# Token rows of a top-2 expert layer: scaled and turned in one fp32 product, with a new order of expert 0's preparation

## The chip, the cores and the metric

One core of a Trainium2 chip runs the kernel in one launch. The metric is the device time of one execution in microseconds (us), as the median of several.

## What is computed

Attention of 4 batches, 8 heads, 768 positions and head size 64, over 96 local and 8 global keys, gives `x` of 3072 tokens by 512. A gate then picks two of eight experts for each token, and each expert is a two-layer network:

```python
noisy_logits = x @ w_gate + np.log1p(np.exp(x @ w_noise)) * noise
...
for e in range(E):                       # 8 experts
    for k in range(2):
        mask = top2[:, k] == e
        h = np.maximum(x[mask] @ w1[e], 0.0)                     # 512 -> 1024
        out[mask] += top2_w[mask, k, None] * (h @ w2[e])         # 1024 -> 512
```

## The kernel before

**Attention** goes over 96 pairs of heads (24 blocks of 128 tokens, four pairs each) in one unrolled loop, `n` (lines 746 to 767). The order of all work is written by hand: an engine takes its instructions in the order in which the program emits them. The table `at(step, function, ...)` hangs other work on the end of a step: loads of weights (`load_w`), the weight scales of expert 0 (`scales(0)`, steps 36 to 70), its first weight matrix (`split(0, 1, j)`, steps 74 to 88) and the first tiles of tokens (`ready(0, t)`, from step 92).

**Routing** (`route`, line 289) goes over five segments of the 24 blocks, woven into the loop. Each ends in scatters that write (token, weight) entries into one list per expert in DRAM, by POOL, two for each block (line 382). After the third segment POOL loads expert 0's list (line 391, tile `tb0`) and gathers its first four tiles of 128 rows (line 219).

**Experts.** Each takes 812 rows: four tiles of 128 (part 0 of `xh`, `xl`) and three of 100 (part 1). Every operand is held as two fp16 parts, a high one and the rest, and a product is three fp16 products. `up(e, c, f)` is one of eight 128-wide slices of the hidden layer for part c (12 matmuls), `down(e, t)` a tile of 128 rows (24 matmuls of 512 columns), `down_t(e, d)` a quarter of the features for all 300 other rows (24 matmuls of 300 columns), and `back` turns the latter to rows again. `put` writes rows out by a POOL scatter (line 807). A generator per expert, `prep(e)`, yields after each step of weight preparation: in `scales` eight maxima on DVE (line 147), a product that turns them (line 151) and one that spreads them (line 159), then 16 `split`s, each an ACT and a DVE step (lines 199, 204). `step(e, n)` advances it, between the products of the expert before.

**Tokens.** `gather` brings a tile of rows (`xg`, five buffers). `ready` (line 230) reduces each row to its sum of magnitudes, makes a power of two from it in four small DVE steps, and writes the scaled row as two fp16 parts, by ACT (line 240) and DVE (line 241), into `xp`. `turn` (line 243) turns these with eight fp16 transposes of 128 (or 100) columns into one PSUM bank; ACT copies the high half to `xh`, DVE the low half to `xl`. `ready` of a tile stands two blocks ahead of its `turn` in experts 1 to 6 (lines 924 to 933), and one ahead in the stretch of `down_t(0, j)` (lines 892 to 899).

Of the kernel before, what the change touches and what calls it, by code (L numbers as in the profile page):

```python
# [20 lines left out]
P = 128  # L21
NP = 96
TA = 4
# [11 lines left out]
def tile_local_global_attention_then_moe(  # L35
# [46 lines left out]
    def bank16(tag, bufs):  # L82
        return psum.tile([P, 1024], F16, name=tag, tag=tag, bufs=bufs)

# [6 lines left out]
    ident16 = consts.tile([P, P], F16, name="ident16")  # L91
    exa = consts.tile([P, E, TA], F32, name="exa")
    exb = consts.tile([MB, E, TB], F32, name="exb")
# [46 lines left out]
    def scales(e):  # L140
# [14 lines left out]
        dg = small.tile([8, 8], F32, name="dg")  # L155
        nc.vector.tensor_scalar(dg, ident[:8, :8], mc, TINY, op0=OP.mult, op1=OP.max)
# [24 lines left out]

    def weigh_a(e):
        nc.vector.scalar_tensor_tensor(yra[:, e], (tba[:, e] if e else tb0)[:, :, 1].bitcast(F32), fac[:, e:e + 1],
                                       exa[:, e], op0=OP.mult, op1=OP.mult)

    def weigh_b(e):
        nc.vector.scalar_tensor_tensor(yrb[:, e], tbb[:, e, :, 1].bitcast(F32), fac[:MB, e:e + 1], exb[:, e],
                                       op0=OP.mult, op1=OP.mult)
# [19 lines left out]
    xg, xp = {}, {}  # L208
# [17 lines left out]
    def spare_bank(make=bank):  # L226
        spare[0] += 1
        return make("m" if spare[0] % 2 else "lg", 1)

    def ready(e, t):  # L230
        x = xg.pop((e, t))
        m = x.shape[0]
        c, s, u = (gp.tile([m, 1], F32, name=f"{n}{m}", bufs=2) for n in ("l1", "pw", "up"))
        ex = exa[:, e, t:t + 1] if t < TA else exb[:, e, t - TA:t - TA + 1]
        nc.vector.tensor_reduce(c, x, op=OP.add, axis=AX.X, apply_absolute_value=True)
        nc.vector.tensor_scalar(c, c, TINY, None, op0=OP.max)
        power(ex, c, s)
        nc.vector.tensor_scalar(u, s, 2.0 ** (X_UP - 1), None, op0=OP.mult)  # L238
        xp[e, t] = gp.tile([m, 2 * Dm], F16, name="xp", bufs=3)
        nc.scalar.activation(xp[e, t][:, :Dm], x, AF.Copy, scale=u)  # L240
        nc.vector.scalar_tensor_tensor(xp[e, t][:, Dm:], x, u, xp[e, t][:, :Dm], op0=OP.mult, op1=OP.subtract)

    def turn(e, t, ps=None):
        x = xp.pop((e, t))
        m = x.shape[0]
        c, c0 = (0, t * P) if t < TA else (1, (t - TA) * MB)
        ps = (spare_bank(bank16) if ps is None else ps)[:, :2 * KC * m].rearrange("p (k t) -> p k t", k=2 * KC)
# [153 lines left out]
    with ExitStack() as actx:  # L401
# [108 lines left out]
        def gate_consts():  # L510
            nc.vector.tensor_copy(ident16, ident)
# [196 lines left out]
        else:  # L708
# [37 lines left out]
            for n in range(NPAIR + LAG):  # L746
# [9 lines left out]
                if n >= NPAIR - 1:  # L756
                    t = n - NPAIR + 1
                    turn(0, t, bank16("sc", 2))
                    if t == 2:
                        turn(0, 3, bank16("sc", 2))  # L760
# [11 lines left out]
    with ExitStack() as mctx:  # L772
# [43 lines left out]
        def down(e, t):  # L816
# [32 lines left out]
        for f in range(FC):  # L849
# [6 lines left out]
            if f == 0:  # L856
                load_w()
# [5 lines left out]
        for t in range(TB):  # L863
            gather(0, TA + t)
        ahead = {e: prep(e) for e in range(1, E)}

        def step(e, n):
# [5 lines left out]
        for t in range(TA - 1):  # L873
            down(0, t)
            step(1, [3, 3, 2][t])
            ready(0, TA + t)
        for t in range(TB):
            turn(0, TA + t, bank16("sc", 2) if t == TB - 1 else None)
        for t in range(3):
            gather(1, t)  # L880
        down(0, TA - 1)
        step(1, 1)
        for f in range(FC):
            up(0, 1, f)
            step(1, 1)
            if f % 2 and f < 6:
                ready(1, f // 2)
                gather(1, 3 + f // 2)
            if f % 2 == 0 and f:
                turn(1, f // 2 - 1)  # L890
        ready(1, 3)
        for j in range(KC):
            down_t(0, j)
            if j == 0:
                gather(1, 6)
            if j < 3:
                ready(1, 4 + j)
            turn(1, 3 + j)
            step(1, 2)
        weigh_b(0)  # L900
        for e in range(1, E):
            last = e + 1 == E
            for f in range(FC):
# [3 lines left out]
                step(e, 4)  # L907
                step(e + 1, 1)
# [15 lines left out]
            for j, (f, t) in enumerate(steps_t + steps if last else steps + steps_t):  # L924
                f(e, t)
                if not last:
                    step(e + 1, [2, 2, 2, 3, 1, 1, 1, 1][j])
                    if j < TA + TB - 2:
                        ready(e + 1, j + 2)
                    if j < TA + TB:  # L930
                        turn(e + 1, j)
                        if j < 2:
                            gather(e + 1, 5 + j)
                elif j in (KC, KC + 1, KC + 2):
# [85 lines left out]
```

## Time and profile before

| | us |
|---|---|
| median of three executions (850.0 to 852.4) | 851.05 |
| the profiled execution | 852.33 |
| its span, first to last instruction | 850.2 |
| TensorE (PE) busy | 782.8 |
| VectorE (DVE) busy | 502.5 |
| ScalarE (ACT) busy | 391.5 |
| GpSimd (POOL) busy | 236.6 |

Busy time of PE contains the latency of each instruction, so what a group costs PE is the time from its start to the start of the next. The clock column of a stretch is the mean granted TensorE clock as a share of 2.4 GHz, and 0.50 is 1.2 GHz. In a timeline the bracket gives the idle time of the engine before the row and what ended it.

### The profile page before, as it was taken

Reading aid. Unit: us, or ns where it says so; the run is one execution under the profiler, and the core shown is the slowest. Engines: PE = TensorE matmul, PEld = TensorE weight load, DVE = VectorE, ACT = ScalarE, POOL = GpSimd, SP = SyncE. Lnnn points to the kernel's source line nnn. Section 1 sums busy time; section 2 is a strip of 40 time slices with the busy share of each in tenths; the row PEclk is TensorE's granted clock in tenths of the full one; section 3 lists DMA queues with packets and bytes.
Section 4 is the critical chain, followed back from the end, with each engine's and each line's share of the span. In section 5 each row is a group of like instructions: output and inputs, shape, how many; then the busy total and the mean of one; then the engine's idle time right before and its main releaser. Section 6 shows DMA issues by size and latency. Waiting matters only on the chain. (4 is left out here: it accounts for less than half of the span.)

```text
span 850.2 us, 14911 instructions
## 1 busy us (share of the span) xinstructions
PE 782.8 (92%) x5513; PEld 535.7 (63%) x5513; DVE 502.5 (59%) x1594; ACT 391.5 (46%) x792; POOL 236.6 (28%) x225
## 2 busy tenths in 40 slices
PE   7999999995598467999999999999999999999994
PEld 6999998995543245465564655656565565665662
DVE  6456766752664557867667666756766766663200
ACT  5777676783341234435424524533542543353211
POOL 4000050586264320404223141240413214122013
PEclk9999999998599599999999999999999999999997
DMA  9899698672436422707423541750643344032014
GB/s 215 230 265 284 180 191 227 166 175 65 134 113 147 83 54 79 201 8 173 114 69 95 162 99 34 185 119 20 160 122 75 94 125 89 7 64 30 1 22 61
DMA packets 86667, 100.77 MB, mean 119 GB/s; under 512 B 35626, under 2 KB 48170, under 8 KB 86586
## 3 DMA queue, kind: packets, MB, share of 16 engines
q1 hardware_dynamic: 71322, 73.05, 31.2%
q0 software_dynamic: 15264, 26.69, 16.8%
q8 instruction: 45, 0.74, 0.4%
q14 instruction: 36, 0.29, 0.1%
HBM read 71.46 MB, written 28.24 MB: 117 GB/s over the span
## 5 line engine op out<-in xcount | busy, mean ns | idle before, releaser
L788 PEld LDWEIGHTS <-w1h 128*128 128x128 f16 x1024 | 100.0, 99 | 70.8 <-issue 0.8
L240 ACT ACTIVATE xp<-xg,up 128x512 f16<-128x512 f32 (+1 forms) x56 | 40.4, 722 | 152.3 <-DVE up L238 109.7
L807 POOL DMA_INDIRECT out_dram<-y,tba x28 | 44.6, 1593 | 234.7 <-ACT y L806 234.7
L822 PE MATMUL av<-w2h,hh 128*128 128x512 f16 x256 | 98.1, 383 | 0.0
L822 PE MATMUL av<-w2l,hh 128*128 128x512 f16 x256 | 98.0, 383 | 0.0
L822 PE MATMUL av<-w2h,hl 128*128 128x512 f16 x256 | 98.0, 383 | 0.0
L572 DVE CUSTOM_DVE_ANT_0 ns<-sc,bias 128x168 f32<-128x168 f32 (+1 forms) x192 | 55.6, 321 | 62.1 <-PE sc L569 31.9
L576 ACT ACTIVATE a<-ns,mx 128x168 f32<-128x168 f32 (+1 forms) x192 | 72.7, 423 | 42.1 <-DVE mx L572 41.4
L382 POOL DMA_INDIRECT tbl<-ent,sli x48 | 48.4, 1008 | 142.0 <-DVE sli L377 129.3
L788 PE MATMUL at<-xh,w1h 128*128 128x512 f16 (+1 forms) x256 | 86.7, 338 | 0.0
L788 PE MATMUL sc<-xh,w1h 128*128 128x512 f16 (+1 forms) x256 | 86.5, 338 | 0.0
L788 PE MATMUL at<-xl,w1h 128*128 128x512 f16 (+1 forms) x256 | 86.3, 337 | 0.0
L788 PE MATMUL sc<-xl,w1h 128*128 128x512 f16 (+1 forms) x256 | 86.2, 337 | 0.0
L788 PE MATMUL at<-xh,w1l 128*128 128x512 f16 (+1 forms) x256 | 86.1, 337 | 0.0
L788 PE MATMUL sc<-xh,w1l 128*128 128x512 f16 (+1 forms) x256 | 86.1, 336 | 0.0
L822 PEld LDWEIGHTS <-hh 128*128 128x128 f16 x512 | 49.8, 99 | 55.3 <-issue 2.2
L807 POOL DMA_INDIRECT out_dram<-y,tbb x24 | 38.1, 1588 | 151.8 <-ACT y L806 151.4
L147 DVE TENSOR_REDUCE wmx<-raw 128x1 f32<-128x1024 f32 x64 | 76.9, 1208 | 0.0
L569 PE MATMUL sc<-ks,qbuf 128*128 128x168 f32 (+1 forms) x384 | 71.0, 310 | 5.6 <-DMA qbuf<-in_q 5.6
L798 ACT ACTIVATE hh<-at 128x300 f16<-128x300 f32 (+1 forms) x62 | 31.3, 505 | 96.5 <-PE at L788 96.5
L832 PE MATMUL av<-hh,w2h 128*128 128x300 f16 x256 | 74.6, 292 | 0.0
L788 PEld LDWEIGHTS <-w1l 128*128 128x128 f16 x512 | 50.2, 98 | 38.5 <-issue 0.5
(163 smaller groups left out, 1623.5 us busy)
## 6 DMA issues: line engine op xcount, KB each, us to landing
raw<-in_w SPq DMA_DIRECT2D x32, 1024.0 KB
out_dram<-zero SPq DMA_DIRECT2D x14, 512.0 KB
vs<-in_v SPq DMA_DIRECT2D x24, 260.0 KB
qbuf<-in_q SPq DMA_DIRECT2D x48, 128.0 KB
xd<-xr SPq DMA_DIRECT2D x24, 256.0 KB
ks<-in_k SPq DMA_DIRECT2D x20, 272.0 KB
vp<-in_v SPq DMA_DIRECT2D x20, 195.0 KB
ks<-in_k SPq DMA_DIRECT2D x4, 464.0 KB
```

The source lines that it names most:

```text
L147: nc.vector.tensor_reduce(m[:, i:i + 1], t[:, i % 2 * n:(i % 2 + 1) * n], op=OP.max, axis=AX.X, apply_absolute_value=True)
L240: nc.scalar.activation(xp[e, t][:, :Dm], x, AF.Copy, scale=u)
L382: ins = nc.gpsimd.indirect_dma_start(out=tbl, out_offset=bass.IndirectOffsetOnAxis(ap=sli[:, i, j:j + 1], axis=0), in_=ent[:, i, j], in_of ...
L569: nc.tensor.matmul(ps[:, s], qs[b, j][:, 2 * i0 + s, hp], ks[b, j][:, hp, k0:k0 + w], start=True, stop=True)
L572: nc.vector.tensor_tensor_reduce(out=ns[:, s, :w], in0=ps[:, s], in1=bias[:, hp, s] if i else bias0[:, hp, s], scale=-scale, scalar=3e38, ...
L576: nc.scalar.activation(A[n][:, s, c:c + w], ns[:, s, :w], AF.Exp, bias=mx[:, s:s + 1], scale=-1.0)
L788: nc.tensor.matmul(ps, w[e % 2][:, k, fs], x[c][:, k], start=n == 0, stop=n == 3 * KC - 1)
L798: nc.scalar.activation(hh[c][:, f], ps, AF.Relu)
L807: ins = nc.gpsimd.indirect_dma_start(out=out, out_offset=bass.IndirectOffsetOnAxis(ap=r[:, 0:1], axis=0), in_=y, in_offset=None, bounds_ch ...
L822: nc.tensor.matmul(ps, x[0][:, f, cols], w[e % 2][:, f], start=n == 0, stop=n == 3 * FC - 1)
L832: nc.tensor.matmul(ps, w[e % 2][:, f, cols], x[1][:, f], start=n == 0, stop=n == 3 * FC - 1)
```

## The change

`ready` no longer makes fp16 parts. After the reduction and two small DVE steps, POOL writes a diagonal matrix `dg`, the identity scaled by the rows' powers of two. `turn` multiplies the gathered fp32 rows with it: four fp32 matmuls, whose result is turned and scaled. ACT takes the high part from PSUM, DVE the rest (PSUM less high part). `xg` is held until `turn`. `scales` loses two of its yields, and so has ten. Expert 0's loads, scales and first weight matrix stand earlier among the attention steps, and the steps around expert 0 and between the experts are in another order.

```diff
@@ scales
         nc.tensor.transpose(ps[:8, :P], m, ident)
-        yield
         mc = small.tile([8, 1], F32, name="mc")
...
-        nc.tensor.matmul(ps[:, :8], one8, dg, start=True, stop=True)
-        yield
+        nc.tensor.matmul(ps[:, :8], one8, d8, start=True, stop=True)
@@ weigh_a and weigh_b
+    def weigh(e, y, c, w):
+        nc.vector.tensor_scalar(c[:, e].bitcast(I32), c[:, e].bitcast(I32), EXP, None, op0=OP.bitwise_and)
+        nc.vector.scalar_tensor_tensor(y[:, e], w.bitcast(F32), fac[:w.shape[0], e:e + 1], c[:, e],
+                                       op0=OP.mult, op1=OP.mult)
@@ ready
-        x = xg.pop((e, t))
+        x = xg[e, t]
...
         nc.vector.tensor_reduce(c, x, op=OP.add, axis=AX.X, apply_absolute_value=True)
         nc.vector.tensor_scalar(c, c, TINY, None, op0=OP.max)
-        power(ex, c, s)
-        nc.vector.tensor_scalar(u, s, 2.0 ** (X_UP - 1), None, op0=OP.mult)
-        xp[e, t] = gp.tile([m, 2 * Dm], F16, name="xp", bufs=3)
-        nc.scalar.activation(xp[e, t][:, :Dm], x, AF.Copy, scale=u)
-        nc.vector.scalar_tensor_tensor(xp[e, t][:, Dm:], x, u, xp[e, t][:, :Dm], op0=OP.mult, op1=OP.subtract)
+        nc.vector.tensor_scalar(s.bitcast(I32), c.bitcast(I32), EXP, EXP, op0=OP.bitwise_and, op1=OP.bitwise_xor)
+        dg[e, t] = gp.tile([m, m], F32, name="dg", bufs=3)
+        nc.gpsimd.tensor_scalar(dg[e, t], ident[:m, :m], s, 2.0 ** (X_UP - 1), op0=OP.mult, op1=OP.mult)
@@ turn
-        for k in range(2 * KC):
-            nc.tensor.transpose(ps[:, k], x[:, k * P:(k + 1) * P], ident16[:m, :m])
+        for k in range(KC):
+            nc.tensor.matmul(ps[:, k], x[:, k * P:(k + 1) * P], d, start=True, stop=True)
         cols = slice(c0, c0 + m)
-        nc.scalar.activation(xh[c][:, :, cols], ps[:, :KC], AF.Copy)
-        nc.vector.tensor_copy(xl[c][:, :, cols], ps[:, KC:])
+        nc.scalar.activation(xh[c][:, :, cols], ps, AF.Copy)
+        nc.vector.tensor_sub(xl[c][:, :, cols], ps, xh[c][:, :, cols])
@@ attention
-            for j in 20, 26, 32, 56, 84, 90:
+            for j in 20, 26, 32, 38, 76, 84, 90:
                 at(j, load_w)
             first = scales(0)
-            for j in 36, 39, 42, 45, 48, 51, 62, 64, 66, 67, 68, 69, 70:
+            for j in 28, 30, 35, 37, 44, 46, 50, 52, 54, 55:
                 at(j, lambda: next(first, 0))
             for j in range(FC):
-                at(74 + 2 * j, split, 0, 1, j, nc.gpsimd)
+                at(56 + 2 * j, split, 0, 1, j, nc.gpsimd)
             for t in range(TA):
-                at(NPAIR - 4 + t, ready, 0, t)
+                at(NPAIR - 3 + min(t, 2), ready, 0, t)
@@ down, and expert 0's up
-        def down(e, t):
+        def down(e, t, between={}):
...
+                    if n in between:
+                        turn(e, between[n], bank("sc", 2) if n > 20 else None)
...
-            if f == 0:
-                load_w()
@@ around expert 0
-        for t in range(TA - 1):
-            down(0, t)
-            step(1, [3, 3, 2][t])
-            ready(0, TA + t)
-        for t in range(TB):
-            turn(0, TA + t, bank16("sc", 2) if t == TB - 1 else None)
-        for t in range(3):
-            gather(1, t)
-        down(0, TA - 1)
-        step(1, 1)
+        for t in range(TA):
+            down(0, t, {13: TA, 18: TA + 1, 22: TA + 2} if t == TA - 1 else {})
+            step(1, 2)
+            if t == TA - 2:
+                for j in range(TB):
+                    ready(0, TA + j)
+        step(1)
+        for t in range(2):
+            ready(1, t)
+        for t in range(2, 5):
+            gather(1, t)
         for f in range(FC):
             up(0, 1, f)
-            step(1, 1)
-            if f % 2 and f < 6:
-                ready(1, f // 2)
-                gather(1, 3 + f // 2)
-            if f % 2 == 0 and f:
-                turn(1, f // 2 - 1)
-        ready(1, 3)
+            if f in (0, 1, 3, 5, 7):
+                step(1)
+            if f in (2, 4):
+                ready(1, 2 + f // 4)
+            if f > 3:
+                turn(1, f - 4)
+                if f < 6:
+                    gather(1, f + 1)
         for j in range(KC):
             down_t(0, j)
-            if j == 0:
-                gather(1, 6)
-            if j < 3:
-                ready(1, 4 + j)
-            turn(1, 3 + j)
-            step(1, 2)
+            step(1)
+            if j < TB:
+                ready(1, TA + j)
+                turn(1, TA + j)
@@ experts 1 to 7, second half of up
             for f in range(FC):
                 up(e, 1, f)
-                step(e + 1, f > 0)
-                if not last and f > 5:
-                    ready(e + 1, f - 6)
+                if f < 2:
+                    step(e + 1)
+                if not last and f in (4, 6):
+                    ready(e + 1, f // 2 - 2)
```

Three places where the instructions move follow. Line numbers of the change are those of its own file, and a number behind a name tells buffers of one name apart.

POOL's queue at the third segment's scatters (`sli_2783` before, `sli_2798` now), expert 0's list (`tb`) and its first gathers. Before:

```order
L382 DMA tbl<-ent_2783,sli_2898 25600x2 x2
L201 TENSOR_SCALAR raw<-raw,wsc 128x4x128
L202 TENSOR_TENSOR w1l_103<-raw,w1h_101 128x4x128
L382 DMA tbl<-ent_2783,sli_2898 25600x2 x8
L391 DMA tb_97<-tbl 128x8
L201 TENSOR_SCALAR raw<-raw,wsc 128x4x128
L202 TENSOR_TENSOR w1l_103<-raw,w1h_101 128x4x128
L201 TENSOR_SCALAR raw<-raw,wsc 128x4x128
L202 TENSOR_TENSOR w1l_103<-raw,w1h_101 128x4x128
L219 DMA xg<-xd,tb_97 128x512 x4
```

Now:

```order
L198 TENSOR_SCALAR raw<-raw,wsc 128x4x128
L199 TENSOR_TENSOR w1l_102<-raw,w1h_100 128x4x128
L377 DMA tbl<-ent_2306,sli_2506 25600x2 x12
L377 DMA tbl<-ent_2798,sli_2910 25600x2 x10
L386 DMA tb_96<-tbl 128x8
L216 DMA xg<-xd,tb_96 128x512 x4
L236 TENSOR_SCALAR dg<-ident,pw_3312 128x128
```

The eight pairs of the weight step (`raw`, `w1l`) that stood among the scatters and behind the list's load now stand ahead of the second and third segments' scatters, and the list's load and the gathers follow the last scatter directly.

DVE's queue at `down_t(0, 0)` to `down_t(0, 1)`: `yt` is the copy of a transposed down product, `w1l` the DVE step of `split`, `xl` the low part of a turn, the reduction of `xg` the first step of `ready`. Before:

```order
L252 COPY xl_106<-lg 128x4x128
L204 SCALAR_TENSOR_TENSOR w1l_104<-raw,wsc,w1h_102 128x4x128 x2
L835 COPY yt<-av 128x300
L235 TENSOR_REDUCE l_4332<-xg 100x1
L236 TENSOR_SCALAR l_4332<-l_4332 100x1
L179 TENSOR_SCALAR exb<-l_4332 100x1
L180 TENSOR_SCALAR pw_4333<-exb 100x1
L238 TENSOR_SCALAR up_4334<-pw_4333 100x1
L241 SCALAR_TENSOR_TENSOR xp<-xg,up_4334,xp 100x512
L252 COPY xl_3496<-m 128x4x100
L204 SCALAR_TENSOR_TENSOR w1l_104<-raw,wsc,w1h_102 128x4x128
```

Now:

```order
L201 SCALAR_TENSOR_TENSOR w1l_103<-raw,wsc,w1h_101 128x4x128
L232 TENSOR_REDUCE l1b<-xg 100x1
L233 TENSOR_SCALAR l1b<-l1b 100x1
L234 TENSOR_SCALAR pw_4191<-l1b 100x1
L247 TENSOR_TENSOR xl_3460<-m,xh_3459 128x4x100
L831 COPY yt<-av 128x300
L201 SCALAR_TENSOR_TENSOR w1l_103<-raw,wsc,w1h_101 128x4x128
L232 TENSOR_REDUCE l1b<-xg 100x1
L233 TENSOR_SCALAR l1b<-l1b 100x1
L234 TENSOR_SCALAR pw_4232<-l1b 100x1
L247 TENSOR_TENSOR xl_3460<-lg,xh_3459 128x4x100
```

Before, `ready` of a tile stands ahead of the `xl` of the tile before it, so that it runs one turn ahead; now each tile's `ready` stands behind the weight step and directly ahead of its own turn.

PE's queue in the second up half of expert 1: `wmx` are the eight maxima of expert 2's weights, `at` and `sc` the banks of slices f = 0 and f = 1. Before:

```order
L788 LDWEIGHTS w1l_104
L788 MATMUL sc<-xh_3495,w1l_104 128x300
L151 MATMUL m<-ident,wmx 8x128
L788 LDWEIGHTS w1h_102
L788 MATMUL at<-xh_3495,w1h_102 128x300
```

Now:

```order
L782 LDWEIGHTS w1l_103
L782 MATMUL at<-xh_3459,w1l_103 128x300
L147 MATMUL m<-ident,wmx 8x128
L782 LDWEIGHTS w1h_101
L782 MATMUL sc<-xh_3459,w1h_101 128x300
```

The product that turns the maxima stood behind slice f = 1 and now stands behind slice f = 0. On DVE the last maximum is still emitted with slice f = 7 of the first half.

## Rows read from the trace of the kernel before

**Rows 1.** The page's part 1: busy us (share of the span) and instructions of each engine, whole span.

```profile
PE 782.8 (92%) x5513; PEld 535.7 (63%) x5513; DVE 502.5 (59%) x1594; ACT 391.5 (46%) x792; POOL 236.6 (28%) x225
```

**Rows 2.** Busy time of each engine in eight stretches: from:to, length, then busy us (instructions) of PE, PEld, DVE, ACT and POOL, the granted TensorE clock as a share of full speed, DMA share, GB/s. The stretches are the last attention steps (200 to 219), the turns of expert 0's first tiles (219 to 233), the first half of expert 0's up projection (233 to 258.4), three of its four down products (258.4 to 274), the turns of its last three tiles and the fourth down product (274 to 298), the second half of its up projection (298 to 322.8), its transposed down products (322.8 to 340.6), and the 500 us of experts 1 to 7 that follow.

```profile
200.00:219.00 19.00, 3.25 (x30) 3.01 (x27) 4.12 (x26) 2.09 (x5) 12.91 (x11) 0.68 0.26 76
219.00:233.00 14.00, 11.47 (x87) 10.74 (x88) 9.16 (x37) 5.93 (x12) 0.00 (x0) 0.50 0.40 132
233.00:258.40 25.40, 24.29 (x121) 11.09 (x121) 17.09 (x64) 11.82 (x22) 16.89 (x16) 0.91 0.36 98
258.40:274.00 15.60, 15.60 (x73) 6.93 (x71) 4.88 (x6) 1.89 (x3) 4.51 (x5) 1.00 0.69 171
274.00:298.00 24.00, 10.72 (x50) 4.83 (x50) 12.52 (x26) 4.60 (x8) 9.41 (x8) 0.64 0.45 89
298.00:322.80 24.80, 16.57 (x125) 11.68 (x124) 14.04 (x39) 9.69 (x18) 5.91 (x5) 0.93 0.21 47
322.80:340.60 17.80, 14.83 (x131) 10.65 (x129) 13.10 (x35) 8.88 (x17) 0.00 (x0) 1.00 0.30 106
340.60:840.60 500.00, 493.90 (x3142) 292.12 (x3139) 301.03 (x635) 204.62 (x365) 125.81 (x94) 1.00 0.38 89
```

**Rows 3.** The timeline of POOL's queue, start us, duration us, engine, line, operation [idle before <-releaser]: the first scatter of the second routing segment, the last scatter of the third, the load of expert 0's list, and the first gather of its rows.

```profile
156.96 0.98 POOL L382 DMA_INDIRECT tbl<-ent,sli  x1 [35.56 <-DVE sli L377]
...
197.79 0.97 POOL L382 DMA_INDIRECT tbl<-ent,sli  x1 [0.30 <-issue]
...
204.07 0.60 POOL L391 DMA_DIRECT2D tb<-tbl  x1 [5.32 <-DMA tbl<-ent,sli]
...
210.47 1.12 POOL L219 DMA_INDIRECT xg<-xd,tb  x1 [0.16 <-issue]
```

**Rows 4.** The timeline of DVE and PE, same columns: the slots of the third segment are ready; the first row of `ready`; PE's first product after its wait; expert 0's first up product.

```profile
177.67 0.17 DVE L377 CAST sli<-sl 128x10 int32<-128x10 f32 x1
...
214.00 0.69 DVE L235 TENSOR_REDUCE l<-xg 128x1 f32<-128x512 f32 x1 [13.88 <-DMA xg<-xd,tb]
...
219.12 0.69 PE L270 MATMUL m<-ident,xr 128*128 128x128 f32 x2 [15.87 <-DVE xr L617]
...
232.98 0.63 PE L788 MATMUL at<-xh,w1h 128*128 128x512 f16 x1
```

**Rows 5.** Groups of instructions of one line and one shape: line, engine, operation, out<-in, shapes, count | busy us, mean ns of one | idle time of the engine before them. Lines 235 and 238 are in `ready`, 147 in `scales`, 199 and 204 the two steps of `split`, 201 its first step on POOL, 799 a read from PSUM less an fp16 part, 837 the copy of a transposed down product.

```profile
L235 DVE TENSOR_REDUCE l<-xg 100x1 f32<-100x512 f32 x24 | 16.3, 678 | 11.2 <-DMA xg<-xd,tbb 11.2
...
L238 DVE TENSOR_SCALAR up<-pw 100x1 f32<-100x1 f32 x24 | 3.7, 153 | 0.8
...
L147 DVE TENSOR_REDUCE wmx<-raw 128x1 f32<-128x1024 f32 x64 | 76.9, 1208 | 0.0
...
L199 ACT ACTIVATE w1h<-raw,wsc 128x512 f16<-128x512 f32 x64 | 44.2, 712 | 0.0
...
L204 DVE SCALAR_TENSOR_TENSOR w1l<-raw,wsc,w1h 128x512 f16<-128x512 f32 x56 | 40.8, 748 | 11.7 <-ACT w1h L199 9.6
...
L201 POOL TENSOR_SCALAR raw<-raw,wsc 128x512 f32<-128x512 f32 x8 | 12.7, 1586 | 0.2
...
L799 DVE SCALAR_TENSOR_TENSOR hl<-sc,hh 128x512 f16<-128x512 f32 x30 | 20.7, 691 | 31.8 <-ACT hh L798 31.8
...
L837 ACT ACTIVATE yt<-av 128x300 f32<-128x300 f32 x16 | 6.6, 414 | 8.4 <-PE av L832 8.4
```

**Rows 6.** The timeline of PE, same columns, in pairs of a group and its successor: an fp16 turn of 128 rows and the next product; one of 100 rows and the next; an fp32 product of 128 columns (two instructions, four records) and the next; an fp32 product of 65 columns with 128x128 weights (one instruction, two records) and the next.

```profile
452.14 0.61 PE L249 MATMUL m<-ident,xp 128*128 128x128 f16 x8
...
452.59 0.38 PE L822 MATMUL av<-w2h,hh 128*128 128x512 f16 x1
...
472.54 0.52 PE L249 MATMUL m<-ident,xp 100*128 100x100 f16 x8
...
472.90 0.29 PE L832 MATMUL av<-hh,w2h 128*128 128x300 f16 x1
...
52.19 0.61 PE L569 MATMUL sc<-ks,qbuf 128*128 128x128 f32 x4
...
52.64 0.33 PE L608 MATMUL av<-vp,at 104*128 104x65 f32 x2
...
194.19 0.39 PE L608 MATMUL av<-vs,at 128*128 128x65 f32 x2
...
194.41 0.39 PE L608 MATMUL av<-vp,at 104*128 104x65 f32 x2
```

**Rows 7.** Waits of PE's weight loads from 360 us to the end: line <- what it waited for: us in total, times, longest.

```profile
PEld L249 <- issue: 5.3, 6, 0.9
...
PEld m L159 <- DVE dg L156: 1.5, 6, 0.2
```

**Rows 8.** The timeline of PE and DVE, same columns, in expert 1: the first product of its second up half, the last of the next expert's eight weight maxima, and the product that turns those maxima.

```profile
434.17 0.29 PE L788 MATMUL at<-xh,w1h 128*128 128x300 f16 x1
...
435.61 1.21 DVE L147 TENSOR_REDUCE wmx<-raw 128x1 f32<-128x1024 f32 x1
...
437.24 0.27 PE L151 MATMUL m<-ident,wmx 128*8 128x128 f32 x1
```

**Rows 9.** The timeline of POOL and PE, same columns: the first gather of expert 0's last three tiles, and the first turn of one of them.

```profile
271.59 1.11 POOL L219 DMA_INDIRECT xg<-xd,tbb  x1 [10.17 <-DMA tbb<-tbl]
...
277.58 0.35 PE L249 MATMUL m<-ident,xp 100*128 100x100 f16 x4 [3.50 <-ACT xp L240]
```

More of the change, by code (lines that the diff above doesn't have):

```diff
@@ L90, in tile_local_global_attention_then_moe @@
     ident = consts.tile([P, P], F32, name="ident")
-    ident16 = consts.tile([P, P], F16, name="ident16")
-    exa = consts.tile([P, E, TA], F32, name="exa")
-    exb = consts.tile([MB, E, TB], F32, name="exb")
+    l1a = consts.tile([P, E, TA], F32, name="l1a")
+    l1b = consts.tile([MB, E, TB], F32, name="l1b")
     wmx = consts.tile([P, 2, 8], F32, name="wmx")
@@ L151, in scales @@
         nc.tensor.transpose(ps[:8, :P], m, ident)
-        yield
         mc = small.tile([8, 1], F32, name="mc")
         nc.vector.tensor_reduce(mc, ps[:8, :P], op=OP.max, axis=AX.X)
-        dg = small.tile([8, 8], F32, name="dg")
-        nc.vector.tensor_scalar(dg, ident[:8, :8], mc, TINY, op0=OP.mult, op1=OP.max)
+        d8 = small.tile([8, 8], F32, name="d8")
+        nc.vector.tensor_scalar(d8, ident[:8, :8], mc, TINY, op0=OP.mult, op1=OP.max)
         yield
         ps = bank("m", 1)
-        nc.tensor.matmul(ps[:, :8], one8, dg, start=True, stop=True)
-        yield
+        nc.tensor.matmul(ps[:, :8], one8, d8, start=True, stop=True)
         m2 = small.tile([P, 2], F32, name="m2")
@@ L206, in split @@
             load_w()
-    xg, xp = {}, {}
+    xg, dg = {}, {}
     def rows(e, t):
@@ L510, in gate_consts @@
         def gate_consts():
-            nc.vector.tensor_copy(ident16, ident)
             nc.vector.memset(one8, 1.0)
@@ L757, in tile_local_global_attention_then_moe @@
                     t = n - NPAIR + 1
-                    turn(0, t, bank16("sc", 2))
+                    turn(0, t, bank("sc", 2))
                     if t == 2:
-                        turn(0, 3, bank16("sc", 2))
+                        turn(0, 3, bank("sc", 2))
                 if LAG <= n:
@@ L864, in tile_local_global_attention_then_moe, with step @@
             gather(0, TA + t)
+        for t in range(2):
+            gather(1, t)
         ahead = {e: prep(e) for e in range(1, E)}
-        def step(e, n):
+        def step(e, n=1):
             for _ in range(n):
@@ L872, in tile_local_global_attention_then_moe @@
         weigh_a(0)
[L873 to L879 removed]
+        for t in range(TA):
[5 more added lines that the diff above has]
+        step(1)
+        for t in range(2):
+            ready(1, t)
+        for t in range(2, 5):
             gather(1, t)
[L881 to L882 removed]
         for f in range(FC):
             up(0, 1, f)
[L885 to L891 removed]
+            if f in (0, 1, 3, 5, 7):
[6 more added lines that the diff above has]
+                    gather(1, f + 1)
         for j in range(KC):
             down_t(0, j)
[L894 to L899 removed]
+            step(1)
+            if j < TB:
+                ready(1, TA + j)
+                turn(1, TA + j)
         weigh_b(0)
@@ L906, in tile_local_global_attention_then_moe @@
                     back(e - 1, f)
-                step(e, 4)
-                step(e + 1, 1)
+                if f < 4:
+                    step(e, 2 if e == 1 else 1)
+                step(e + 1)
             if not last:
@@ L915, in tile_local_global_attention_then_moe @@
                 up(e, 1, f)
-                step(e + 1, f > 0)
-                if not last and f > 5:
-                    ready(e + 1, f - 6)
+                if f < 2:
+                    step(e + 1)
+                if not last and f in (4, 6):
+                    ready(e + 1, f // 2 - 2)
             if not last:
@@ L926, in tile_local_global_attention_then_moe @@
                 if not last:
-                    step(e + 1, [2, 2, 2, 3, 1, 1, 1, 1][j])
                     if j < TA + TB - 2:
@@ L933, in tile_local_global_attention_then_moe @@
                             gather(e + 1, 5 + j)
+                    step(e + 1, 2 if j < TA else 1)
                 elif j in (KC, KC + 1, KC + 2):
```

20 lines of the change are left out of this document (8 added, 12 removed).

## The prediction

> **What bounds the kernel.** I read the page's part 1 first: TensorE is busy for 782.8 of 850.2 us [rows 1], so the kernel is a TensorE kernel, and the question is where its 67 idle us lie and what the change adds to the busy ones. The windows by stage answer the first part [rows 2]. The 500 us of experts 1 to 7 hold only 6 idle us, at full clock; the 140 us from 200 to 340.6 hold some 43, and in three of those stretches the granted clock is 0.50 to 0.68. So work that is added to PE in experts 2 to 7 is paid in full, and work on DVE, ACT or POOL there costs nothing unless PE waits for it; around expert 0 the chain of waits sets the time, and each wait is followed by PE at 1.2 instead of 2.4 GHz.
>
> Then I followed that chain in the timelines. POOL's scatters of the second routing segment start at 156.96 although the slots of the third are ready at 177.67; POOL is busy with weight steps and scatters in between, ends the last scatter at 198.8, waits 5.3 us for its landing, loads the list at 204.07, and gathers at 210.47 [rows 3, 4]. DVE, in order, stands at the first `ready` for 13.9 us until 214.0, and the last attention pairs behind it on DVE leave PE empty for 15.9 us, until 219.1 [rows 4]. PE then turns and multiplies at half clock for 14 us [rows 2] and starts expert 0's first product at 232.98 [rows 4].
>
> All terms are against the profiled execution: 852.33 us, of which 850.2 are span. It lies 1.3 above the median of 851.05, and I take that off at the end.
>
> **The turns, experts 2 to 7 (42 tiles, inside the 500 us).** An fp16 turn of 128 rows holds PE for 0.45 us, one of 100 rows for 0.36 [rows 6]. The new turn is four fp32 products of 128 (or 100) columns. The trace has two of 128 columns in 0.45, or 0.223 each, and one of only 65 columns in 0.22 [rows 6]: fewer columns were no cheaper, so I price both widths at 0.223, and a turn at 0.89. That is +0.44 for 24 tiles and +0.53 for 18, together +20.1. If cost went by columns, a turn of 100 rows would be 4 x 0.223 x 100/128 = 0.70, and the term 16.7.
>
> The Trainium skill (FP8 and Floating Point Precision, TensorE Precision Notes) says that true fp32 takes four passes through the array. By that a product of 100 columns is four times 100 columns at 2.4 GHz, an estimate of 0.167 us, and the term some 4 us smaller; the 65-column row speaks against it here, since by the same rule it would last 0.11 and it lasts 0.22.
>
> The lighter `ready` and the heavier `xl` lie beside PE. A tile loses an ACT pass (about 0.71), a DVE pass (about 0.75) and two small steps (0.15 each); its `xl` becomes a read of fp32 PSUM, as in a row of 0.69 [rows 5]. DVE is busy for 301 of 500 us, ACT for 205 [rows 2], so nothing is gained by it. `dg` is new on POOL, bounded by its 128x512 step of 1.59 and a quarter of it, 0.4 [rows 5]; it stands behind row scatters in a queue that is busy for a quarter of the stretch [rows 2], but two blocks of PE work ahead of its turn, so I cost it at nothing. Without that cover it would be 0.4 to 1.6 a tile.
>
> **The waits of the steady state.** PE waits six times for 0.9 us at a turn of 100 rows, 5.3 in all, where the bank still holds a tile that `xl` has not read; with `ready` shorter and spread wider this goes: -5.3. The 0.2-us waits at the product that spreads the scales [rows 7] go too, -1.5, as its two parts no longer stand a slice apart with PE behind them. But the product that turns the maxima now stands behind slice f = 0. In expert 1 that slice starts at 434.17; 12 products at the pitch of 0.128 end it at 435.71, and the last maximum ends at 435.61 + 1.21 = 436.82 [rows 8]. PE, in order, waits 1.1 us, six times: **+6.6**. Its bounds: 0 if DVE, with less to do, is 1.1 us earlier; 9 if `ready` work ahead of it makes it half a microsecond later. Steady sum: 20.1 - 5.3 - 1.5 + 6.6 = **+19.9** (10 to 23).
>
> **End of attention.** With the weight steps out of the way, POOL runs the 12 scatters from 156.96 at the present pitch of about 1.29, to 172.4, waits for the slots at 177.8, and runs ten more to 190.7 instead of 198.8: 8 us. The same 5.3 of landing puts the list load at 196, the gathers, 6.4 behind it as now, at some 202, perhaps 199 since two weight pairs no longer stand between, and the first tile, 3.5 behind its gather, at 202.7 to 206 [rows 3, 4]. `ready` also stands a pair later in the loop. So DVE's wait shrinks from 13.9 to 3 or less, PE's from 15.9 likewise, and the 14 us at half clock [rows 2] run nearer to full. First product at about 213 instead of 233: **-20** (bounds: -14, if scatter landings hold the list to 199; -23, if the clock never falls). Moving the loads, scales and splits earlier I cost at nothing: those steps lie beside attention pairs on DVE and ACT; if they are not covered, the eight maxima of 1.21 [rows 5] bound it at 10, shared by the same eight at their old place, so it is a difference of 1 or 2.
>
> **From the first product to expert 1's first, now 107.6 us (233 to 340.6).** The first half of `up` keeps its length, less 2 for the first products at full clock. Then, now, three downs run, PE waits for the last three tiles (10.2 us of POOL waiting for its list, first turn at 277.58 [rows 9]), and the clock is 0.64 [rows 2]. In the new order all four downs run through, with the three turns inside the fourth. The tiles are gathered some 40 us after the first product; three `ready`s of 0.68 + 2 x 0.15 and a `dg` each are done before the fourth down's 13th product. Downs end at about 47, a wait of 3 follows at the product that turns the maxima (its maxima stand behind three `xl` on DVE), and eight slices of 1.54 with four turns of 0.89 end near 66. Now the same point is at 322.8 - 233 = 89.8 [rows 2, 4]: 24 us gained.
>
> The four transposed downs give part of this back. Now they take 17.8 [rows 2], with each tile's `ready` a turn ahead. In the new order `ready` stands behind `yt` and the weight step and directly ahead of its turn, and PE has nothing between: for the first, `yt` 0.41, `w1h` 0.71, `w1l` 0.75, `ready` 1.0, `dg` 0.4 [rows 5] and the hops, about 3.7 us; 2.9 and 3.7 for the next two. That is 10.3 of waits, 4 x 3.06 of products (24 of 0.128) and 3 x 0.89 of turns, or 25.2; and after such waits the clock fell in every stretch of [rows 2] that has them, so I add 1.65 to each of three downs, about 5 (bounds 0 and 10). Expert 1 starts at some 96.3 after the first product instead of 107.6: **-11.3** (-18 to -6).
>
> **Sum.** +19.9 - 20 - 11.3 = -11.4: span 838.8, run 840.9, at the median's level **839.6**, so 840. The tail after expert 7 is the same code. Best ends of all terms give 820, worst 853.
>
> **Rivals.** *Slower: the turns are paid and the list is no earlier.* If the scatters' landings, and not POOL's issues, set when the list can be read, the first gather stays near 210. Then DVE's wait keeps some 11 of its 13.9, PE's wait and the cold turns stay, and -20 becomes about -4: 851.05 + 19.9 - 4 - 11.3 = 856. Between a first gather at 200 (-20) and one at 210 (-4) I go in a line; it decides from 207, where the sum is zero. Against it: POOL's last scatter ends 8 us later than its slots allow, and the 5.3 us of landing is short [rows 3]; for it: 22 scatters run without a break now, and the rows show none so. Chance 0.12. *Faster: no wait gives anything back.* If the clock stays up in the transposed downs (-5), 100-row turns cost 0.70 (-3.4) and no maximum is late (-2 of the 6.6), it is 830. For it: PE waits of 3 us with 3 us of work between are shorter than those behind which the clock fell. Chance 0.18. *No change: the transposed downs run at half clock throughout.* The stretch 274 to 298 shows a stage with waits of that kind, 10.7 busy of 24.0 at 0.64 [rows 2]. Products and turns of 14.9 would take 14.9 more, of which 5 are in the sum: 10 more, 850. Chance 0.10. That the change fails to do what it says I hold at nothing: the orders shown have the moves.
>
> **Numbers.** Forecast 0.60, which leaves rivals 0.40 as above. A measurement tells about 0.3% (848.5 to 853.6) from no change. Slower than that takes the first rival and its neighbours, 0.13; within it the third rival, 0.10; faster the rest, 0.77. The range, 824 to 853, leaves out the first rival and the best few of the second's bounds.
>
> **What would show it.** Right: no DVE wait of over 3 us at the first row reduction and no empty 16 us on PE; the first gather near 200; turns as groups of eight fp32 records that hold PE for 0.89; expert 1's first product near 309 and the 500 us behind it some 520 long; PE waits of about 1.1 before the product that turns the maxima, and of 3 to 4 at the turns among the transposed downs. Wrong: a first gather at 207 or later; a turn much shorter than 0.8; a stretch of experts 1 to 7 outside 510 to 523; waits at turns of experts 2 to 7 behind `dg`, which would show as POOL on PE's path.

## The result: slower by 1.2%, where faster was forecast

| | before | the change |
|---|---|---|
| median (us) | 851.72 (850.0 to 854.13, 4 runs) | 863.37 (858.65 to 863.72, 4 runs) |
| ratio, 95% interval | | 1.0122 (1.0078 to 1.0165) |
| span of the profiled execution | 850.2 | 861.5 |
| PE busy | 782.8 | 808.1 |

The forecast was 840 in a range of 824 to 853. The page of the change begins:

```profile
PE 808.1 (94%) x5513; PEld 563.8 (65%) x5513; DVE 467.7 (54%) x1441; ACT 362.5 (42%) x736; POOL 263.8 (31%) x281
```

Read against [rows 1]: PE has 25 us more, DVE and ACT 35 and 29 less, with the same 5513 instructions on PE. The windows of the change, cut at its own stages (attention's end; expert 0's first up half; its downs up to the first turn; the rest of them; second up half; transposed downs; 500 us of experts 1 to 7), answer to [rows 2]:

```profile
200.00:213.16 13.16, 12.05 (x117) 11.05 (x117) 10.01 (x50) 6.23 (x13) 3.13 (x6) 1.00 0.44 159
213.16:239.49 26.33, 23.98 (x121) 10.72 (x121) 18.83 (x65) 11.94 (x22) 17.88 (x17) 0.94 0.41 116
239.49:257.84 18.35, 18.35 (x86) 8.23 (x84) 10.13 (x15) 2.58 (x4) 6.02 (x6) 1.00 0.66 145
257.84:274.43 16.59, 8.07 (x36) 5.90 (x35) 2.42 (x7) 1.93 (x4) 6.09 (x7) 0.69 0.47 78
274.43:294.10 19.67, 16.56 (x133) 13.36 (x133) 14.93 (x36) 8.12 (x17) 8.80 (x10) 1.00 0.32 72
294.10:328.01 33.91, 24.31 (x122) 17.18 (x120) 8.61 (x19) 5.58 (x11) 1.05 (x3) 0.70 0.09 32
328.01:828.01 500.00, 493.42 (x3041) 304.23 (x3039) 275.23 (x524) 179.11 (x317) 139.21 (x129) 1.00 0.38 88
```

The half clock at the end of attention is gone (1.00 where [rows 2] had 0.68 and 0.50). Expert 0 has it in two stretches: 257.8 to 274.4, with half of PE empty, at 0.69 (before, 274 to 298 at 0.64), and, new, the transposed downs, 33.9 us at 0.70 where they took 17.8 at 1.00. The last stretch is as full as before, with 3041 instructions of PE in 500 us instead of 3142.

The terms, measured against forecast in the same profiled executions:

| term | forecast | measured |
|---|---|---|
| first product of expert 0 (233.0 before) | -20 | -19.8 (213.16) |
| from there to expert 1's first product (107.6 before) | -11.3 | +7.3 (114.9) |
| experts 1 to 7, first to last product (497.6 before) | +19.9 | +22.3 (519.9) |
| behind the last product | 0 | +1.6 |
| sum | -11.4 | +11.4 |

So 18.6 of the 22.8 us of error lie in one term, expert 0's own stage: 11.7 in its downs and the wait behind them, 3.7 in the transposed downs, 2.9 in the first up half and the rest in the second. POOL's queue at the end of attention, against [rows 3]:

```profile
158.78 1.04 POOL L377 DMA_INDIRECT tbl<-ent,sli  x1 [0.16 <-issue]
...
189.75 0.97 POOL L377 DMA_INDIRECT tbl<-ent,sli  x1 [0.30 <-issue]
...
194.67 0.60 POOL L386 DMA_DIRECT2D tb<-tbl  x1 [3.95 <-DMA tbl<-ent,sli]
...
196.94 1.07 POOL L216 DMA_INDIRECT xg<-xd,tb  x1 [1.66 <-DMA tb<-tbl]
```

The list is read at 194.67 and the first gather starts at 196.94, 13.5 earlier than before; 196 and 199 to 202 were forecast. Then POOL, ACT, DVE and PE around expert 0's last three tiles, against [rows 9]. First POOL:

```profile
251.57 1.12 POOL L216 DMA_INDIRECT xg<-xd,tbb  x1 [11.01 <-DMA tbb<-tbl]
...
257.11 1.01 POOL L216 DMA_INDIRECT xg<-xd,tba  x1 [0.30 <-issue]
258.42 1.65 POOL L801 DMA_INDIRECT out_dram<-y,tb  x1 [0.30 <-issue]
260.37 1.59 POOL L801 DMA_INDIRECT out_dram<-y,tb  x1 [0.31 <-issue]
264.51 1.55 POOL L801 DMA_INDIRECT out_dram<-y,tb  x1 [2.55 <-ACT y L800]
265.54 1.55 POOL L236 TENSOR_SCALAR dg<-ident,pw 100x100 f32<-100x100 f32 x3
```

ACT, the second and third `y` of the row scatters:

```profile
250.05 0.69 ACT L800 ACTIVATE y<-av,yra 128x512 f32<-128x512 f32 x1 [4.49 <-PE av L816]
263.55 0.69 ACT L800 ACTIVATE y<-av,yra 128x512 f32<-128x512 f32 x1 [12.81 <-DMA out_dram<-y,tb]
```

DVE, the powers of two of the three tiles, and PE:

```profile
256.22 0.15 DVE L234 TENSOR_SCALAR pw<-l1b 100x1 int32<-100x1 int32 x1
...
258.00 0.15 DVE L234 TENSOR_SCALAR pw<-l1b 100x1 int32<-100x1 int32 x1
...
266.50 0.15 DVE L234 TENSOR_SCALAR pw<-l1b 100x1 int32<-100x1 int32 x1 [6.83 <-POOL dg L236]
```

```profile
266.52 2.03 PE L244 MATMUL m<-dg,xg 100*128 100x100 f32 x8 [8.52 <-POOL dg L236]
268.34 0.63 PE L816 MATMUL av<-w2l,hh 128*128 128x512 f16 x1
...
277.70 0.27 PE L147 MATMUL m<-ident,wmx 128*8 128x128 f32 x1 [3.11 <-DVE wmx L143]
...
300.69 2.03 PE L244 MATMUL m<-dg,xg 100*128 100x100 f32 x8 [3.40 <-POOL dg L236]
...
310.44 2.03 PE L244 MATMUL lg<-dg,xg 100*128 100x100 f32 x8 [2.73 <-POOL dg L236]
...
321.16 2.03 PE L244 MATMUL m<-dg,xg 100*128 100x100 f32 x8 [3.46 <-POOL dg L236]
```

Read from the end: the first turn waits 8.52 for `dg`. DVE had its power at 256.37, before PE wanted the turn (at some 257.8), but `dg` stands on POOL behind the scatter at 264.51, which waits for its `y`. ACT could not write that `y` for 12.81 us, because both `y` buffers were held by scatters that POOL issued only at 258 to 260: it had stood for 11 us at expert 0's second list and then issued five gathers. A turn at half clock then takes 1.8 (266.52 to 268.34).

### The profile page after: what moved, and what is told of

Its sections match the earlier page's. It is cut to its first block, busy times and chain, and to the rows that moved or that the text cites. A ratio compares the mean times of both kernels' runs of the same rounds, so it can differ in the third digit from the quotient of the medians.

```text
span 861.5 us, 14844 instructions
## 1 busy us (share of the span) xinstructions
PE 808.1 (94%) x5513; PEld 563.8 (65%) x5513; DVE 467.7 (54%) x1441; ACT 362.5 (42%) x736; POOL 263.8 (31%) x281
## 5 line engine op out<-in xcount | busy, mean ns | idle before, releaser
L236 POOL TENSOR_SCALAR dg<-ident,pw 128x128 f32<-128x128 f32 (+1 forms) x56 | 36.0, 654 | 172.3 <-DVE pw L234 161.1
L828 PE MATMUL av<-hh,w2h 128*128 128x300 f16 x256 | 77.6, 303 | 0.0
L828 PE MATMUL av<-hh,w2l 128*128 128x300 f16 x256 | 76.9, 300 | 0.0
L828 PE MATMUL av<-hl,w2h 128*128 128x300 f16 x256 | 76.8, 300 | 0.0
L801 POOL DMA_INDIRECT out_dram<-y,tbb x24 | 38.3, 1595 | 125.5 <-ACT y L800 125.2
L800 ACT ACTIVATE y<-av,yra 128x512 f32<-128x512 f32 x32 | 22.0, 687 | 127.9 <-issue 61.5
```

What stands on the lines that cost most here:

```text
L236: nc.gpsimd.tensor_scalar(dg[e, t], ident[:m, :m], s, 2.0 ** (X_UP - 1), op0=OP.mult, op1=OP.mult)
L800: nc.scalar.activation(y, ps, AF.Copy, scale=w)
L801: ins = nc.gpsimd.indirect_dma_start(out=out, out_offset=bass.IndirectOffsetOnAxis(ap=r[:, 0:1], axis=0), in_=y, in_offset=None, bounds_ch ...
L828: nc.tensor.matmul(ps, w[e % 2][:, f, cols], x[1][:, f], start=n == 0, stop=n == 3 * FC - 1)
```

## The experiments

The experiments ran in three series, each with runs of the kernel before of its own, and that kernel stood at two levels: a lower one, 850 to 854, in the result above and in the third series, and a higher one, 865 to 870, in the first and second. The run records name the same chip for the first and the third series, so it is not the chip as such. Where the expectations say "chip", read "series". The profile of the kernel before in the second series shows where the difference lies: its span is 13.6 longer, its first product of expert 0 is at 247.0 against 233.0, and its experts take 71.55 each as before. So stages are compared across series from that product on, and what lies ahead of it at one level only. One stage varies even so: the transposed downs of the change, with nearly the same waits, took 28.6 to 34.1 in the kernels that left them alone. All stage times, from the starts of the first products of each stage in PE's timeline:

| kernel, series | median, ratio to before (95%) | first product | up, 1st half | downs | up, 2nd half | transposed | per expert 1 to 6 |
|---|---|---|---|---|---|---|---|
| before | 851.7 | 233.0 | 25.4 | 39.6 | 24.8 | 17.8 | 71.55 |
| the change | 863.4, 1.0122 | 213.2 | 26.3 | 38.3 | 16.2 | 33.9 | 75.2 |
| order_only, 1 | 881.6, 1.0175 (1.0148 to 1.0202) | 248.2 | 25.3 | 36.7 | 20.6 | 34.0 | 71.9 |
| turn_only, 1 | 867.4, 1.0009 (0.999 to 1.0028) | 240.9 | 26.3 | 33.0 | 22.7 | 16.4 | 74.0 |
| dg_dve, 1 | 887.8, 1.0196 (1.0156 to 1.0236) | 246.2 | 26.3 | 29.5 | 17.8 | 34.1 | 75.2 |
| max_later, 1 | 882.4, 1.0167 (1.0143 to 1.0191) | 242.1 | 24.7 | 39.0 | 17.8 | 31.5 | 74.0 |
| before_same_chip, 2 | 865.9 (one run), series 867.5 | 247.0 | 25.4 | 39.3 | 24.4 | 17.8 | 71.55 |
| after_same_chip, 2 | 891.6, 1.0284 (1.0263 to 1.0306) | 244.0 | 26.3 | 38.8 | 17.8 | 28.6 | 75.2 |
| dt_early, 2 | 873.9, 1.0063 (1.0044 to 1.0082) | 241.7 | 24.6 | 39.0 | 17.8 | 15.2 | 75.2 |
| best, 2 | 849.9, 0.9773 (0.9749 to 0.9797) | 250.4 | 27.0 | 30.3 | 20.6 | 14.8 | 70.7 |
| filler, 3 | 854.7, 1.0041 (1.0022 to 1.0061) | 213.2 | 26.3 | 38.6 | 16.2 | 25.4 | 75.2 |
| table_only, 3 | 840.0, 0.9855 (0.9839 to 0.9871) | 220.2 | 25.3 | 39.4 | 24.6 | 17.8 | 71.6 |
| best2, 3 | 819.3, 0.9617 (0.9604 to 0.9631) | 219.4 | 25.3 | 27.8 | 25.2 | 14.8 | 70.7 |
| repaired, 3 | 829.0, 0.9737 (0.9714 to 0.976) | 213.5 | 24.6 | 30.7 | 17.6 | 15.0 | 74.0 |

**One half of the change at a time.** order_only puts the old turn into the changed order:

```diff
-        dg[e, t] = gp.tile([m, m], F32, name="dg", bufs=3)
-        nc.gpsimd.tensor_scalar(dg[e, t], ident[:m, :m], s, 2.0 ** (X_UP - 1), op0=OP.mult, op1=OP.mult)
+        nc.vector.tensor_scalar(u, s, 2.0 ** (X_UP - 1), None, op0=OP.mult)
+        nc.scalar.activation(xp[e, t][:, :Dm], x, AF.Copy, scale=u)
+        nc.vector.scalar_tensor_tensor(xp[e, t][:, Dm:], x, u, xp[e, t][:, :Dm], op0=OP.mult, op1=OP.subtract)
...
+            nc.tensor.transpose(ps[:, k], x[:, k * P:(k + 1) * P], ident16[:m, :m])
```

> The change with the old turn (fp16 parts by ACT and DVE, eight fp16 transposes), everything else as changed. Theory: the new turn costs PE 20 us in experts 2 to 7 and the order of expert 0 gives some 12; without the new turn about 844 us. The 8.5-us wait at the first turn inside the fourth down stays nearly as long, because ACT's part of ready stands behind the same row scatter's y (PE gap of 7 to 9 there). Rival: the fp32 turns are cheap and the order itself is what costs: 858 or more. Second rival: the wait at the turn is POOL's alone (dg), and goes without it: about 833.

turn_only is the opposite: before with the change's `ready`, `turn` and `weigh`.

> The kernel before with the new ready and turn alone, its order kept. Theory: +20 us of PE in experts 2 to 7, less some 4 of the old waits at the third 100-row turn, plus waits for dg behind row scatters around expert 0: 866 to 874, say 869. Rival (turns cheap, order costs): 850 to 856.

Both totals missed, and not only because the level of the series was 16 higher: order_only, expected 7 below before, is 14 above it in its own series, and turn_only, expected some 18 above, is level with it. By these totals the order costs and the turn does not, as the rivals had it; neither half was run alone at the lower level. By stage they say more. An expert takes 71.55 before, 74.0 with the new turn, 71.9 with the new order and 75.2 with both. The new turn costs 2.45 an expert, 14.7 in six, and about as much comes back around expert 0: there turn_only has no wait for fp16 parts, and its downs are 6.6 shorter than before, its second up half 2 and its first product 6 earlier than that of before in the second series, which is of the same level. In order_only that product gains nothing (248.2 against 247.0), and the way from it to expert 1 is 9 longer (116.6 against 107.6). The first expectation's last guess was decided too: the wait of expert 0's fourth down is not POOL's alone. With the old `ready`, ACT's part stands behind the same `y`, and PE waits nearly as long (ACT and PE in order_only):

```profile
298.85 0.69 ACT L807 ACTIVATE y<-av,yra 128x512 f32<-128x512 f32 x1 [14.04 <-DMA out_dram<-y,tb]
299.44 0.71 ACT L241 ACTIVATE xp<-xg,up 100x512 f16<-100x512 f32 x1
```

```profile
300.21 0.51 PE L250 MATMUL m<-ident,xp 100*128 100x100 f16 x4 [8.14 <-ACT xp L241]
```

**The queue in front of `dg`.** dg_dve moves one instruction to another engine:

```diff
-        nc.gpsimd.tensor_scalar(dg[e, t], ...)
+        nc.vector.tensor_scalar(dg[e, t], ...)
```

> The change with dg made by DVE and not POOL. Theory: the fourth down's first turn waited only because dg stood on POOL behind the third down's row scatter, which waits for its y, which waits for a buffer that earlier scatters hold. With dg on DVE that wait of 8.5 us goes, with 2 to 3 us of half clock behind it, and each of the three waits among the transposed downs is 0.6 shorter: about 850. Rival: the tiles land too late for the turn anyway, and 5 us or more of the wait stay: 857 to 860.

PE's waits from 215 to 355 in dg_dve:

```profile
PE m L244 <- issue: 6.5, 2, 3.2
PE m L147 <- DVE wmx L143: 5.9, 1, 5.9
PE lg L244 <- issue: 2.5, 1, 2.5
```

No wait of 8.5 to 9.3 is left; the downs take 29.5, against 38.8 of the change in the second series. The theory of the queue holds: without the wait for the maxima the downs take 23.6, which is what the prediction gave them (their end at 47, less a first up half of 23.4). But 2.8 of the gain go to the next wait (5.9 for the maxima, 3.1 in the change), and the three waits among the transposed downs stay (3.2, 2.5, 3.2): they are not POOL's, the hop I had put at 0.6 each is hardly there. The total cannot show it: its runs reach from 878 to 977, and its series has no run of the change.

**The maxima.** max_later:

```diff
-                if f < 2:
+                if f in (1, 2):
                     step(e + 1)
```

> The change with the two steps behind slices f = 1 and 2 of each second up half, so that the product that turns the maxima stands where it stood before. Theory: the six waits of 1.1 us go, nothing takes their place: 856.8, 6.6 less than the change. Rival: the work of the scales is then late and a later product waits as long: 862 to 864.

74.0 an expert instead of 75.2 (73.99 and 75.25): six times 1.26, or 7.5, and the view of PE's waits lists none in experts 1 to 7, where the change has this one alone:

```profile
PE m L147 <- DVE l1a L177: 6.6, 6, 1.1
```

The total, 882.4 where 856.8 was expected, is of the higher level and has no run of the change beside it.

**The same series for both.** Nothing is edited here.

> The kernel before, for its trace on the chip of these runs. In the runs so far it took 851 on one chip and 868 on another. Theory: its 16.5 more there lie ahead of expert 0's first product, in waits of ScalarE and VectorE in the attention section that no instruction of the program ends; from expert 1 to the end it takes 509.6 as on the first chip. Rival: the slower chip is slower throughout.

> The change itself, beside the kernel before on the same chip. On the first chip it was 12 slower. Theory: from expert 0's first product on it is 7.3 - 12 slower as on the first chip (114.9 against 107.6 up to expert 1, +22 behind), whatever the chip; ahead of that product the chip decides what is gained: 20 where it has no such waits, little or nothing where it has. So 863 where before takes 851, and 884 to 892 where before takes 868. Rival: the ratio is the same on each chip, 1.012.

As expected: all of before's difference lies ahead of the first product, and the change gains 3 there instead of 20, so that it is 24 slower. ACT's waits from 60 to 245 in before_same_chip have what the trace of before has not (the first line); the second line is DVE's first row of `ready` there:

```profile
ACT ls L281 <- remote: 11.2, 2, 5.9
```

```profile
227.30 0.69 DVE L235 TENSOR_REDUCE l<-xg 128x1 f32<-128x512 f32 x1 [0.38 <-DMA xg<-xd,tb]
```

This row tells why most of the gain is gone. Against [rows 4] it starts 13.3 later and waits 0.38 instead of 13.88, so DVE's work ahead of it ends 26.8 later: before hides half of that delay in its wait for expert 0's rows. The change has no such wait left to hide a delay in. Of the 17 us that are missing from the gain this wait is 13.5.

**The transposed downs.** dt_early takes the waits away, filler only fills them:

```diff
+        ready(1, TA)
         for j in range(KC):
+            if j + 1 < TB:
+                ready(1, TA + j + 1)
             down_t(0, j)
             step(1)
             if j < TB:
-                ready(1, TA + j)
                 turn(1, TA + j)
```

> The change with each ready of the transposed downs of expert 0 one turn earlier. Theory: the three waits of 3.4, 2.7 and 3.5 us go, and with them the stretches at half clock behind them (8.8): the four transposed downs take some 16 to 18 and not 34, the kernel 16 to 18 less than the change on the same chip. Rival: the clock falls there for another reason, and only the 9.6 of waits go.

```diff
+        if fill is not None:
+            for i in range(24):
+                nc.tensor.matmul(fill, w2h[0][:, i % FC, :P], hh[1][:, i % FC], start=True, stop=True)
         for k in range(KC):
             nc.tensor.matmul(ps[:, k], x[:, k * P:(k + 1) * P], d, start=True, stop=True)
...
-                turn(1, TA + j)
+                turn(1, TA + j, fill=bank("sc", 2)[:, :CB])
```

> The change with 24 more products of 128x300 on PE ahead of each of the three turns among expert 0's transposed downs, into a bank that nothing reads: some 3 us of work in waits of 2.7 to 3.5 us, nothing else changed. Theory: the granted clock falls because PE stands empty there; with the filler it stays at 1.00, and the four transposed downs, waits included, take about 25 (28.6 to 34.1 so far). Rival: the waits alone cost, the filler only adds to them: 34 or more.

The windows of the stage, dt_early first, then filler:

```profile
323.10:338.40 15.30, 15.26 (x123) 12.11 (x123) 8.57 (x19) 5.57 (x11) 1.05 (x3) 1.00 0.20 70
```

```profile
294.30:319.60 25.30, 24.60 (x194) 18.96 (x192) 8.63 (x19) 5.58 (x11) 1.04 (x3) 1.00 0.13 43
```

Both theories hold. Without the waits the stage takes 15.2 and not 28.6 in the same series; the kernel is 17.7 faster, as expected, but some 4 of these lie ahead of the stage, in parts that the edit leaves alone. With 72 useless products in the waits it takes 25.4 where the change, in a series of the same level, takes 33.9: 8.5 us were half clock alone, and the whole kernel is 8.7 faster (854.65 against 863.37, the other stages up to the last product being equal to 0.3) with more work.

**The attention order alone.** table_only is before with the change's steps for loads, scales, splits and `ready` in the attention loop.

> The kernel before with the change's order in the attention section alone (loads, scales and first splits of expert 0 earlier, ready a pair later); turn and the order around expert 0 as before. Theory, where the kernel before takes 851: POOL's list is read 9 us earlier and expert 0's first product starts near 213 to 218 and not 233: 832 to 837. Where it takes 868, the waits of ScalarE and VectorE ahead take the place of that gain: first product at 243 to 250 against 247, 864 to 870. Rival: the gain of 20 came from the new ready and turn and not from the order: 848 or more on the first kind of chip.

Faster by 1.5%, 840 where 832 to 837 was expected: the order gives 12.8 of the 19.8 at the first product (220.2). The other 7 come with the new `ready` and `turn`, so the rival holds in part, and my first theory had too much. Between 200 and 222 PE runs at a granted clock of 0.65 in table_only, and at 1.00 in filler, which is the change up to there:

```profile
200.00:222.00 22.00, 16.45 (x121) 13.73 (x121) 14.84 (x71) 8.33 (x17) 1.35 (x2) 0.65 0.26 93
```

```profile
200.00:222.00 22.00, 20.54 (x164) 15.08 (x164) 14.59 (x65) 9.15 (x19) 8.72 (x12) 1.00 0.57 197
```

best2, with the new order and the old turn, starts at 219.4, repaired, with the new turn, at 213.5.

**Repairs.** best is order_only with the edits of dt_early and max_later, and `ready` of expert 0's last tiles one down earlier; best2 moves one `step(1)` behind the first slice of expert 0's second up half; repaired is dg_dve, max_later and dt_early together.

> The order of the change with the old fp16 turn, the maxima's product a slice later, ready of expert 0's last three tiles one down earlier, and those of the transposed downs one turn earlier. Theory, from the terms: an expert takes 70.7 (71.9 with the old turn and the changed order, less the 1.2 of the maxima), 26 for the four downs, 16 to 18 for the transposed ones: 43 us less than the change on the same chip, 30 less than the kernel before where before takes 851. Rival: the waits move elsewhere; no more than 20 less than the change.

> The version so far best (850 where before takes 867.5) with the product that turns expert 1's maxima behind the first slice of expert 0's second up half, not ahead of it. Theory: its wait of 4.6 us shrinks to 3 or less, no half clock behind it: 846 on that chip. Rival: the next step waits instead, no gain.

> The change with its fp32 turn kept and its three waits taken away together: dg made by DVE, the maxima's product a slice later, ready of the transposed downs a turn earlier. Theory, from single edits on the chip where before takes 867.5: 107.8 - 18.8 = 89 from expert 0's first product to expert 1's first (111.6 in the change), 74.0 an expert: 891.6 - 22.6 - 7.3 = 862. It stays above the version with the old turn by six times 3.3. Rival: the edits overlap, 870 or more.

The first came out (42 less than the change in its series, 43 expected), though its downs took 30.3 where 26 was expected. repaired is 34 below the change at its level (863.4), where 30 were expected: nothing shows that the edits overlap. The total of best2 cannot be set beside that of best, being of another series, but its wait did pass on, to the product that spreads the scales (3.3), so the rival holds: from the first product to expert 1 it takes 93.2 against 92.8. Still it is the fastest kernel here, 0.9617 (0.9604 to 0.9631) of before. The edits add up: 71.9 - 1.2 = 70.7 an expert with the old turn, 74.0 with the new.

## Why the prediction was wrong

- **End of attention, -20: right in size, in part by luck.** It is -19.8, and POOL's queue moved as described. But the prediction gave all of it to the order, at least 14, and the order alone is worth 12.8 (table_only); the other 7 came with the new `ready` and `turn`, for which it had no term here.
- **Turns, +20.1: right.** best2 and repaired differ in experts 1 to 6 by `ready` and the turn alone: 74.0 - 70.7 = 3.3, six times 3.3 is 19.8. The two widths cost nearly the same, as the 65-column row said. The Trainium skill (FP8 and Floating Point Precision, TensorE Precision Notes) gives true fp32 four passes through the array, by which a turn of 100 rows would take an estimate of 0.67 at 2.4 GHz. This trace does not bear that estimate out: it has 0.87. A turn of 128 rows (369.28 to 370.17) and one of 100 (391.45 to 392.32) in the change:

```profile
369.28 1.05 PE L244 MATMUL m<-dg,xg 128*128 128x128 f32 x8
370.17 0.38 PE L816 MATMUL av<-w2h,hh 128*128 128x512 f16 x1
...
391.45 1.03 PE L244 MATMUL m<-dg,xg 100*128 100x100 f32 x8
392.32 0.29 PE L828 MATMUL av<-hh,w2h 128*128 128x300 f16 x1
```

- **Waits of the steady state, -6.8 and +6.6: nearly.** Those at the third 100-row turn gave 3.3 - 2.45 = 0.85 an expert, 5.1; the 1.5 at the spread of the scales stayed; the maxima cost 7.5.
- **Expert 0's stage, -11.3: wrong, +7.3.** The step that failed is the sentence that "three `ready`s ... and a `dg` each are done before the fourth down's 13th product". The first `ready` was (256.4) and the second nearly (258.2), the `dg`s were not: POOL wrote them from 265.5 on. I had costed `dg` at nothing by POOL's load and its distance in the steady state, and never followed the queue in which it stands around expert 0: three row scatters, a `y` that needs a buffer, gathers and a list that lands at 251.6. The rows had it: [rows 9] shows POOL standing 10 us at that list. Downs and the maxima behind them took 38.3 where I had 26.6. The wait itself was 8.5, half clock behind it the rest, some 3. With `dg` on DVE all of it goes, and 9.3 are left of the gain, since the maxima are then waited for 2.8 longer (dg_dve).
- The half clock among the transposed downs was forecast at 5, bounds 0 and 10; it was 8.5 (filler). The waits, forecast at 10.3, are 9.6. The first up half, forecast 2 shorter, is 0.9 longer: PE waits 2.0 for routing there, and the clock falls behind it (0.94).
- None of the rivals was this one. The slower one put its doubt on the scatters of the lists, where nothing was wrong. A slip in the range changes nothing of this: the worst ends of the terms add up to 854, not 853.

## What to carry to other kernels

Before a small new instruction is costed at nothing, walk its in-order queue back, at each place where it is issued, to the last thing that waits there, and ask for the buffers that its neighbours need: a load of a quarter says nothing of the queue at one spot. A chain of short waits in a stage is paid twice, once empty and once at half clock, so it is worth moving useful work into it. Where PE is full for hundreds of us, what an edit adds per round is paid in full, adds up to within 0.1 us, and can be read from one round. A gain that comes out of a wait is worth no more than the wait: at the higher level, where most of it was gone already, 20 us became 3.

## What the runs showed of the hardware

- After each of the three PE waits of 2.7 to 3.5 us among the transposed downs of the change, the turn took 1.8 and not 0.87, and most products of the next down ran at a pitch of 0.25 and not 0.128 (granted clock of the stage 0.70); with the waits filled the clock stayed at 1.00 (filler). In the second series the same waits cost less (0.88, 28.6 us): what the clock takes differs between executions with the same waits.

```profile
326.95:355.55 28.60, 19.00 (x123) 13.65 (x121) 8.64 (x19) 5.61 (x11) 1.05 (x3) 0.88 0.10 37
```

- At the higher level ACT and DVE stop together in the attention section for up to 7.3 us (ACT in the change, second series), with no instruction or transfer in the profile that ends it ("remote"). ACT's stops add up to 14.6 us before and 14.3 in the change there, and expert 0's first product comes 14 and 31 later, so they are not shown to be all of the delay. Why two series had them and the others not stays open.
